# Chunk bounds with the keys held still and the queries streamed, and a scheduler with a table of priority shifts

## Chip, cores, metric

One core of a Trainium2 chip runs the whole program. The metric is device time in microseconds (us); a kernel's time is the median of its runs. The engines are TensorE (PE, with its weight loads shown apart as PEld), VectorE (DVE), ScalarE (ACT), GpSimd (POOL) and SyncE (SP), which here only issues DMAs.

## What is computed

For 4 batches and 8 heads, sequence 768, head size 64, attention is restricted to 6 of 24 key chunks per query. The chunks are chosen by an upper bound from the chunk's minimum and maximum keys. The result feeds a phase mixer of width 512.

```python
k_min = np.min(k_chunks, axis=3)
k_max = np.max(k_chunks, axis=3)
ub = np.sum(np.maximum(q[:, :, :, None, :] * k_min[:, :, None, :, :], q[:, :, :, None, :] * k_max[:, :, None, :, :]), axis=-1)
ub = np.where(causal, ub, -1000000000.0)
top_chunks = np.argsort(ub, axis=-1)[..., -top_k:]
...
theta = x @ w_theta
zr = x * cos_t
zi = x * sin_t
yr = np.einsum('ts,bsd->btd', w_tok_r, zr)
yi = np.einsum('ts,bsd->btd', w_tok_i, zi)
u = x + (yr + yi)
return (u + np.maximum(u @ w_ch, 0.0))
```

## The kernel before, in words

The work of a batch falls into two groups of four heads, 8 groups in all. For one group:

- **tree** (`keys`, L334 to L342): DVE takes the maximum and the minimum of the keys of each chunk, in three steps each. PE transposes the two results (psk, L355) and DVE writes them with signs into the fp32 tile `bnd` (L360): for either sign `y`, a column per head and chunk, with zeros in the 64 rows that belong to the other head of a pair.
- **kext**: POOL casts the keys (L367), PE transposes them (pkt, L375), ACT or DVE copies them out (L381).
- **queries** (L404, L412, L414): PE transposes two heads' queries in fp32 (psq); ACT or DVE writes the positive and the negative part into `ubq`, fp32, for the 5 blocks of 128 queries that need a choice. The blocks come in two parts, of 2 and of 3 (`PARTS`).
- **choice** (L433 to L464): PE multiplies the queries by `bnd`. For each block, pair of heads and sign there is one fp32 matmul: the 128 query columns are the stationary operand, the 48 columns of `bnd` stream. The result, psub, has queries on its partitions. DVE adds the causal mask (ubs, L440), finds the 8 largest of 24 per head (L450) and writes the selection into `qe` (L455). Two transposing DMAs turn `qe` into `qext` (L464).
- **scores, av, norm** (L500 to L545) for each head: PE computes scores (psc), ACT the exponentials (pt), POOL the triangular mask, PE the product with the values (psav), DVE the division into `x16`.

A batch then has transposes of x16 (psT), **phases** (pst L590, cosine and sine on ACT L598, product zz on DVE L604), the **mixer** (psy, in the last batch also psz, L630 and L632: 12 matmuls of 512 columns for each of 6 token tiles; u on DVE L642) and the **output** (a transpose of u, on PE as psut L652 with a copy uT L656, or by DMA L646; pso L664; ot L669; a DMA to the output).

The kernel writes no order by hand. Each piece is a task with an engine (or two that may take it), a duration, a key and its buffers, and `Plan.order` plays the tasks through a list scheduler: whichever engine can start first takes, of the tasks that can start at once, the one with the smallest key. The program is emitted in that order, and each engine runs its instructions in it. `LAT` is the latency that the scheduler adds behind a task of an engine. PSUM has 2 buffers "sc" for scores, 1 "av" and 3 "mi"; psk, pkt, psq, psub, psT, pst, psy, pso and the rest share the three.

The matmul of the bounds is this:

```python
for a in range(nb):
    for z, u in enumerate(us):
        c = slice(z * 2 * NCH, (z + 1) * 2 * NCH)
        for y in range(2):
            nc.tensor.matmul(t[:, a, c], st[u][:, y, (i0 + a) * P:(i0 + a + 1) * P],
                             bnd[g][:, y, c], start=(y == 0), stop=(y == 1))
```

Of the kernel before, what the change touches and what calls it, by code (L numbers as in the profile page):

```python
# [16 lines left out]
class Task:  # L17
    __slots__ = ("i", "eng", "dur", "fn", "key", "deps", "succ", "alloc", "uses", "opts", "lock", "psum",
                 "after_start", "left", "ready", "start", "end", "kind")


class Plan:
# [8 lines left out]
    LAT = {"PE": 0.15, "ACT": 0.20, "DVE": 0.12, "POOL": 0.15, "SP": 2.0}  # L31

    def __init__(self, bufs, in_order, hot, boost):
        self.tasks = []
        self.bufs = bufs
        self.in_order = in_order
        self.count = {}
        self.hot, self.boost = hot, boost
        self.turn = {}
        self.writers, self.readers = {}, {}  # L40
        self.tag_of, self.users = {}, {}

    def add(self, eng, dur, key, fn, r=(), w=(), new=(), after=(), kind=None, lock=False):
# [3 lines left out]
        t.lock = lock or eng == "POOL"  # L47
        t.deps, t.after_start, t.succ, t.alloc, t.uses = set(), set(), [], [], []
# [142 lines left out]
def kernel(  # L191
# [41 lines left out]
    for t in range(2):  # L233
# [18 lines left out]
    bnd = [per.tile([P, 2, 96], FP32, name=f"bnd{i}", tag=f"bnd{i}") for i in range(2)]  # L252
# [8 lines left out]
        "v32": ([P, 2, NT, D], FP32, 2), "mm": ([96, 192], FP32, 1), "h1": ([96, 24, D], FP32, 1),  # L261
        "ubq": ([P, 2, NM * P], FP32, 4), "ubs": ([P, NM, 4, NCH], FP32, 1), "top8": ([P, NM, 4, 8], FP32, 1),
# [3 lines left out]
        "cs": ([P, 2, dm], FP16, 2), "ot": ([P, dm], FP32, 2),  # L266
    }
# [6 lines left out]
    plan = Plan({**{t: s[2] for t, s in SIZE.items()}, **PSUM}, set(SIZE), set(PSUM), BOOST)  # L274
# [24 lines left out]
    def load_kc(b, g, key):  # L299
        n = ("kc", b, g)  # L300

        for c in range(4):
# [4 lines left out]
            dma(key, 196608, 280, go, w=[(n, c)], nw=[n] if c == 0 else [])  # L307

    def load_q(b, p, key):
        n = ("q32", b, p)  # L310
# [6 lines left out]
    def load_v(b, g, y, key):  # L317
        n = ("v32", b, g, y)
# [8 lines left out]
    def keys(b, g, key, wait, lead):  # L327
        kc, mm, psk = ("kc", b, g), ("mm", b, g), ("psk", b, g)
        rk = [(kc, c) for c in range(4)]
        for i, op in ((0, ALU.max), (1, ALU.min)):  # L330
# [5 lines left out]
            def quarter(op=op, hn=hn):  # L336
                h1 = st[hn]
                nc.vector.tensor_tensor(out=h1[:, 16:24, :], in0=h1[:, 0:8, :], in1=h1[:, 8:16, :], op=op)  # L338

            def red(i=i, op=op, hn=hn):  # L340
                t = new(mm) if i == 0 else st[mm]
                nc.vector.tensor_reduce(out=t[:, i * D:(i + 1) * D],  # L342
                                        in_=st[hn][:, 16:24, :].rearrange("p w d -> p d w"), axis=AX.X, op=op)
# [6 lines left out]
        plan.add("POOL", 0.25, key - 0.5, dup, r=[(mm, 0)], w=[(mm, 2)])  # L350
# [8 lines left out]
        def ev():  # L359
            nc.vector.tensor_tensor(  # L360
                out=bnd[g].rearrange("p i (h j c) -> p i h j c", h=4, c=4),
                in0=st[psk].rearrange("p i (c h j) -> p i h j c", c=4, h=4),
                in1=signs[:, 2:194].rearrange("p (i h j c) -> p i h j c", i=2, h=4, c=4), op=ALU.mult)
        plan.add("DVE", dve_t(192), key, ev, r=[(psk, 0), "signs"], w=[("bnd", g)])
        for a in (0, 16):
            def cast(a=a):
                nc.gpsimd.tensor_copy(out=ke[:, a:a + 16, :], in_=st[kc][:, a:a + 16, :])  # L367
            plan.add("POOL", 1.1, key, cast, r=rk, w=[("ke", a)])
# [19 lines left out]
    def queries(b, p, key):  # L388
        q32, g, x0 = ("q32", b, p), p // 2, 2 * (p % 2)
# [5 lines left out]
        plan.add("POOL", 0.9, key, cast, r=rq + ["qe0"], w=[("qe", x0, "q")])  # L395
# [24 lines left out]
    def choice(b, g, key):  # L420
        ubs, top8 = ("ubs", b, g), ("top8", b, g)
        for i, blocks in enumerate(PARTS):
# [4 lines left out]
            def mm(i0=i0, nb=nb, psub=psub, us=us):  # L427
                t = newp(psub, "mi", [P, nb, 4 * NCH], FP32)
                for a in range(nb):
                    for z, u in enumerate(us):  # L430
                        c = slice(z * 2 * NCH, (z + 1) * 2 * NCH)
                        for y in range(2):
                            nc.tensor.matmul(t[:, a, c], st[u][:, y, (i0 + a) * P:(i0 + a + 1) * P],  # L433
                                             bnd[g][:, y, c], start=(y == 0), stop=(y == 1))
            plan.add("PE", 0.13 * 4 * nb, key, mm, r=[("bnd", g)] + [(u, i, z) for u in us for z in range(2)],
                     w=[(psub, 0)], new=[(psub, "mi")])

            def add(i0=i0, nb=nb, psub=psub, i=i):
                t = new(ubs) if i == 0 else st[ubs]
                nc.vector.tensor_tensor(out=t[:, i0:i0 + nb], in0=st[psub].rearrange("p a (x c) -> p a x c", c=NCH),  # L440
                                        in1=cmask32[:, i0:i0 + nb].unsqueeze(2).broadcast_to([P, nb, 4, NCH]),
                                        op=ALU.add)
            plan.add("DVE", dve_t(nb * 96), key, add, r=[(psub, 0), "cmask"], w=[(ubs, i)],
# [27 lines left out]
    def values(b, g, key):  # L471
        for y in range(2):
# [10 lines left out]
    def attend(b, h, key, act_after):  # L483
        g, x = h // 4, h % 4
# [38 lines left out]
        psav = ("psav", b, h)  # L523
        for i, ts in enumerate(([0, 1, 2], [3, 4], [5])):
# [11 lines left out]
        rec, xx = ("rec", b, h), ("x16", b)  # L536
        rp = [(psav, i) for i in range(3)]
# [18 lines left out]
    def transpose16(src, dst, c, key, reads, by_dma):  # L556
        pst = ("psT",) + dst + (c,)
        if by_dma:
            def tp():
                if c == 0:  # L560
                    new(dst)
                nc.sync.dma_start_transpose(out=st[dst][:, c, :].rearrange("p (a t) -> p a t", t=P),
                                            in_=st[src][:, :, c * P:(c + 1) * P].rearrange("p a d -> p (a d)"))
            raise NotImplementedError

# [13 lines left out]
    def phases(b, key, act_after):  # L579
        xx, xT, zz = ("x16", b), ("xT16", b), ("zz", b)  # L580
        act = []
# [228 lines left out]
```

## Time and profile before

| | |
|---|---|
| median of 3 runs | 307.36 us (306.66 to 308.02) |
| the profiled execution | 305.35 us |
| its span on the core | 303.5 us |
| PE busy | 262.7 us, 87% |
| DVE busy | 194.2 us, 64% |
| ACT busy | 152.7 us, 50% |
| POOL busy | 134.7 us, 44% |
| mean share of the DMA engines, queue 1 | 60.9% |

The span runs from the first to the last instruction that the profiler saw; the execution's own time is 1.85 us longer. Busy time of PE counts the modelled length of matmuls that overlap, so it is an upper reading. Shares over the span hide that the program has parts with different limits: loads and trees at first, the attention of the first two batches with the weights' loads, then two batches with few loads, and a last mixer with nothing beside it.

### The profile page before, as it was taken

Reading aid. Unit: us, or ns where it says so; the run is one execution under the profiler, and the core shown is the slowest. Engines: PE = TensorE matmul, PEld = TensorE weight load, DVE = VectorE, ACT = ScalarE, POOL = GpSimd, SP = SyncE. Lnnn points to the kernel's source line nnn. Section 1 sums busy time; section 2 is a strip of 40 time slices with the busy share of each in tenths; the row PEclk is TensorE's granted clock in tenths of the full one; section 3 lists DMA queues with packets and bytes.
Section 4 is the critical chain, followed back from the end, with each engine's and each line's share of the span. In section 5 each row is a group of like instructions: output and inputs, shape, how many; then the busy total and the mean of one; then the engine's idle time right before and its main releaser. Section 6 shows DMA issues by size and latency. Waiting matters only on the chain.

```text
span 303.5 us, 5732 instructions
## 1 busy us (share of the span) xinstructions
PE 262.7 (87%) x2168; PEld 181.6 (60%) x2168; DVE 194.2 (64%) x460; ACT 152.7 (50%) x213; POOL 134.7 (44%) x179
## 2 busy tenths in 40 slices
PE   0279599998699799899989699999999999889993
PEld 0169397697487357786675256866784676544441
DVE  0854925967968996968987825873776344443083
ACT  0421723776525498912545876915539875543010
POOL 2641254976854756987440435917300555200000
PEclk9999999999986999999997979999999999999999
DMA  7991794994996999899799414337207222110014
GB/s 133 200 187 36 129 186 79 240 195 87 250 210 180 245 258 212 237 220 188 199 201 197 112 54 105 51 74 147 62 2 174 37 75 66 54 52 35 0 47 163
DMA packets 90611, 40.81 MB, mean 134 GB/s; under 512 B 83880, under 2 KB 84136, under 8 KB 89816
## 3 DMA queue, kind: packets, MB, share of 16 engines
q1 hardware_dynamic: 90584, 40.45, 60.9%
q8 instruction: 17, 0.28, 0.4%
q14 instruction: 10, 0.08, 0.1%
HBM read 26.28 MB, written 6.29 MB: 107 GB/s over the span
## 4 chain that ended last, share of the span: by engine, by line
PE 62%; DVE 20%; DMA 6%; ACT 6%; issue 2%; POOL 2%; SPq 0%; DVEq 0%; POOLq 0%; ACTq 0%
PE psub L433 15%; PE psc L500 10%; PE psy L630 6%; PE psy L632 6%; PE psav L530 6%; PE pso L664 5%; DVE h L338 4%; PE pst L590 4%; DVE h L334 4%; DVE mm L342 3%; ACT pt L509 3%; DMA kc<-in_k_dram 2%; DVE zz L604 2%; PE psT L571 2%; DVE ot L669 2%
## 5 line engine op out<-in xcount | busy, mean ns | idle before, releaser
L509 ACT ACTIVATE pt<-psc 128x1024 f16<-128x1024 f32 (+1 forms) x96 | 82.8, 917 | 47.2 <-PE psc L500 46.2
L520 POOL TENSOR_TENSOR pt<-pt,tri 128x256 f16<-128x256 f16 x96 | 66.8, 711 | 60.8 <-ACT pt L509 60.6
L500 PE MATMUL psc<-qext,kext 88*128 88x512 f16 (+3 forms) x256 | 55.7, 337 | 8.5 <-DMA qext<-qe 4.2
L500 PEld LDWEIGHTS <-kext 88*128 88x128 f16 x256 | 34.2, 154 | 23.0 <-issue 12.6
L630 PE MATMUL psy<-zz,wtokT 128*128 128x512 f16 x120 | 46.5, 387 | 1.3 <-ACT cs L598 1.0
L433 PE MATMUL psub<-bnd,ubq 128*128 128x48 f32 x320 | 46.7, 314 | 0.8 <-DVE ubq L414 0.6
L433 PEld LDWEIGHTS psub<-bnd,ubq 128*128 128x128 f32 x320 | 46.0, 232 | 1.7 <-PE psc L500 0.8
L632 PE MATMUL psy<-zz,wtokT 128*128 128x512 f16 x120 | 46.4, 387 | 0.0
L530 PEld LDWEIGHTS <-pt 128*128 128x128 f16 x672 | 28.7, 101 | 5.2 <-issue 0.4
L530 PE MATMUL psav<-v,pt 128*128 128x65 f16 x672 | 30.3, 197 | 0.1
L664 PE MATMUL pso<-wch,uT 128*128 128x512 f16 x96 | 24.8, 389 | 4.0 <-DMA uT<-u 1.7
L412 ACT ACTIVATE ubq<-psq,signs 128x256 f32<-128x256 f32 (+1 forms) x39 | 18.6, 523 | 18.2 <-DVE ubq L414 9.7
L334 DVE TENSOR_TENSOR h<-kc 96x1024 f32<-96x1024 f32 x16 | 20.8, 1300 | 9.1 <-DMA kc<-in_k_dram 8.9
L404 PE MATMUL psq<-ident,q 128*128 128x128 f32 x80 | 15.8, 317 | 11.6 <-DMA q<-in_q_dram 10.3
L590 PE MATMUL pst<-wtheta,xT 128*128 128x512 f16 x96 | 23.8, 389 | 2.1 <-ACT cs L598 1.7
L669 DVE SCALAR_TENSOR_TENSOR ot<-pso,u 128x512 f32<-128x512 f32 x24 | 16.4, 689 | 14.1 <-PE pso L664 11.9
L367 POOL CAST ke<-kc 96x1024 f16<-96x1024 f32 x16 | 18.3, 1159 | 12.9 <-DMA kc<-in_k_dram 9.6
L440 DVE TENSOR_TENSOR ubs<-psub,cmask 128x192 f32<-128x192 f32 (+1 forms) x16 | 6.5, 407 | 27.2 <-PE psub L433 27.2
L598 ACT ACTIVATE cs<-pst,pi 128x512 f16<-128x512 f32 x24 | 16.9, 705 | 13.4 <-PE pst L590 7.3
L632 PEld LDWEIGHTS <-wtokT 128*128 128x128 f16 x144 | 14.3, 99 | 15.4 <-issue 3.7
L604 DVE TENSOR_TENSOR zz<-x,cs 128x1024 f16<-128x1024 f16 x24 | 19.2, 813 | 6.4 <-ACT cs L598 6.4
L630 PEld LDWEIGHTS <-wtokT 128*128 128x128 f16 x144 | 14.3, 99 | 13.9 <-issue 1.2
(49 smaller groups left out, 340.4 us busy)
## 6 DMA issues: line engine op xcount, KB each, us to landing
kc<-in_k_dram SPq DMA_DIRECT2D x32, 192.0 KB
q<-in_q_dram SPq DMA_DIRECT2D x32, 192.0 KB
v<-in_v_dram SPq DMA_DIRECT2D x64, 96.0 KB
out_dram<-ot SPq DMA_DIRECT2D x24, 256.0 KB
w<-in_moe_w_tok_r_dram SPq DMA_DIRECT2D x6, 384.0 KB
w<-in_moe_w_tok_i_dram SPq DMA_DIRECT2D x6, 384.0 KB
w<-in_moe_w_theta_dram SPq DMA_DIRECT2D x4, 256.0 KB
w<-in_moe_w_ch_dram SPq DMA_DIRECT2D x4, 256.0 KB
```

The lines of the kernel that those rows point to most:

```text
L334: nc.vector.tensor_tensor(out=new(hn)[:, 0:16, :], in0=st[kc][:, 0:16, :], in1=st[kc][:, 16:32, :], op=op)
L433: nc.tensor.matmul(t[:, a, c], st[u][:, y, (i0 + a) * P:(i0 + a + 1) * P], bnd[g][:, y, c], start=(y == 0), stop=(y == 1))
L500: nc.tensor.matmul(t[:, a0:a1], kx[0:KX, hj:CH * 96:NCH], qx[0:KX, q0 + a0 - o:q0 + a1 - o], start=True, stop=True)
L509: nc.scalar.activation(out=t[:, BASE[s]:BASE[s] + wa + wb], in_=st[psc][:, 0:wa + wb], func=AF.Exp, bias=0.0, scale=scale)
L520: nc.gpsimd.tensor_tensor(out=d, in0=d, in1=tri16.unsqueeze(1).broadcast_to([P, 2, P]), op=ALU.mult)
L530: nc.tensor.matmul(t[:, a, :], st[pt][:, o:o + P], v16s[g][:, x, j, :], start=(j == 0), stop=(j == a))
L590: nc.tensor.matmul(p, st[xT][:, c, t * P:(t + 1) * P], wtheta16[:, c, :], start=(c == 0), stop=(c == 3))
L604: nc.vector.tensor_tensor(out=st[zz][:, t, :, :], in1=st[cs], op=ALU.mult, in0=st[xx][:, t, :].unsqueeze(1).broadcast_to([P, 2, dm]))
L630: nc.tensor.matmul(acc(), wtokT16[:, i, 0, t * P:(t + 1) * P], st[zz][:, i, 0, :], start=(i == 0), stop=False)
L632: nc.tensor.matmul(acc(), wtokT16[:, i, 1, t * P:(t + 1) * P], st[zz][:, i, 1, :], start=False, stop=(i == NT - 1))
L664: nc.tensor.matmul(p, st[uT][:, c, :], wch16[:, c, :], start=(c == 0), stop=(c == 3))
L669: nc.vector.scalar_tensor_tensor(out=new(ot), in0=st[pso], scalar=0.0, op0=ALU.max, in1=st[u][:, t, :], op1=ALU.add)
```

## The change

Four edits.

1. The matmul of the bounds changes sides. `bnd` becomes a tile with 32 columns per head, of which 24 are used and 8 stay zero (a memset at the start). For each part, pair of heads and sign, 64 columns of `bnd` are the stationary operand and the part's 256 or 384 query columns stream. One pair of heads writes PSUM partitions 0 to 63, the other 64 to 127. A group has 8 such matmuls where it had 20.
2. The result now has chunks on its partitions, so it is copied to SBUF in fp32 (`ubm`, by ACT or DVE), transposed on PE in blocks of 128 (`psut` in `choice`, 5 for a group), and the mask is added from there.
3. Every task belongs to a named stage of a batch and group, and a table SHIFT adds a number to its key. Five latencies and several durations of the scheduler change. So the order of the whole program changes.
4. The tile h1 of the tree shrinks from 24 to 16 rows of chunks: its second step writes over its first rows.

```diff
-    LAT = {"PE": 0.15, "ACT": 0.20, "DVE": 0.12, "POOL": 0.15, "SP": 2.0}
+    LAT = {"PE": 0.22, "ACT": 0.08, "DVE": 0.08, "POOL": 0.08, "SP": 2.0}
...
+        t.key += self.shift.get(self.group, 0.0)
+        t.group = self.group
...
-    bnd = [per.tile([P, 2, 96], FP32, name=f"bnd{i}", tag=f"bnd{i}") for i in range(2)]
+    bnd = [per.tile([P, 2, 4, 32], FP32, name=f"bnd{i}", tag=f"bnd{i}") for i in range(2)]
...
+    SHIFT = {
+        ('av', 0, 0): 12.75, ('av', 0, 1): 16.25, ('av', 1, 0): -4.25, ('av', 1, 1): 2, ('av', 2, 0): 0.25,
...
-            dma(key, 196608, 280, go, w=[(n, c)], nw=[n] if c == 0 else [])
+            dma(key, 196608, 172, go, w=[(n, c)], nw=[n] if c == 0 else [])
...
-                nc.vector.tensor_tensor(out=h1[:, 16:24, :], in0=h1[:, 0:8, :], in1=h1[:, 8:16, :], op=op)
+                nc.vector.tensor_tensor(out=h1[:, 0:8, :], in0=h1[:, 0:8, :], in1=h1[:, 8:16, :], op=op)
...
+            c0, w = i0 * P, nb * P
+            ubm, psut = ("ubm", b, g), ("psut", b, g, i)
+
+            def mm(c0=c0, w=w, psub=psub, us=us):
+                t = newp(psub, "mi", [P, w], FP32)
+                for y in range(2):
+                    for z, u in enumerate(us):
+                        nc.tensor.matmul(t[64 * z:64 * z + 64, :],
+                                         bnd[g][:, y, 2 * z:2 * z + 2, :].rearrange("p x c -> p (x c)"),
+                                         st[u][:, y, c0:c0 + w], start=(y == 0), stop=(y == 1))
...
+            def cp(e, c0=c0, w=w, psub=psub, i=i):
+                t = new(ubm) if i == 0 else st[ubm]
+                (nc.scalar.copy if e == "ACT" else nc.vector.tensor_copy)(out=t[:, c0:c0 + w], in_=st[psub])
...
+            def tr(i0=i0, nb=nb, psut=psut):
+                t = newp(psut, "mi", [P, nb, P], FP32)
                 for a in range(nb):
...
+                    nc.tensor.transpose(t[:, a, :], st[ubm][:, (i0 + a) * P:(i0 + a + 1) * P], ident32)
...
+                nc.vector.tensor_tensor(
+                    out=t[:, i0:i0 + nb], in0=st[psut].rearrange("p a (x c) -> p a x c", c=32)[:, :, :, 0:NCH],
+                    in1=cmask32[:, i0:i0 + nb].unsqueeze(2).broadcast_to([P, nb, 4, NCH]), op=ALU.add)
...
+        for i in range(2):
+            nc.vector.memset(bnd[i], 0.0)
```

Three places show how the order moves. The first is PE at the bounds of the second group of batch 0 (psub from `bnd_76`). Before:

```order
L355 MATMUL psk<-ident_58,mm 128x96 x2
L500 LDWEIGHTS kext_67
L500 MATMUL psc<-qext_69,kext_67 128x512
L500 LDWEIGHTS kext_67
L500 MATMUL psc<-qext_69,kext_67 128x256
L500 LDWEIGHTS kext_67
L500 MATMUL psc<-qext_69,kext_67 128x256
L433 MATMUL psub<-bnd_76,ubq 128x48 x20
L530 LDWEIGHTS pt
L530 MATMUL psav<-v_0_73,pt 128x65
```

Now:

```order
L566 MATMUL psc<-qext_69,kext_67 128x384
L484 MATMUL psub<-ubq,bnd_76 64x256 x4
L484 MATMUL psub<-ubq,bnd_76 64x384 x4
L499 MATMUL psut<-ident_58,ubm 128x128 x2
L566 LDWEIGHTS kext_67
L566 MATMUL psc<-qext_69,kext_67 128x512
L566 LDWEIGHTS kext_67
L566 MATMUL psc<-qext_69,kext_67 128x128
L566 LDWEIGHTS kext_67
L566 MATMUL psc<-qext_69,kext_67 128x512
```

Twenty fp32 matmuls are replaced by eight wider ones and by transposes; scores of heads stand between the transposes of the first part and those of the second, while in the first group of all (not shown) the five transposes stand directly behind the eight matmuls.

The second is DVE at the same place. Before:

```order
L360 TENSOR_TENSOR bnd_76<-psk,signs 128x192
L440 TENSOR_TENSOR ubs<-psub,cmask_61 128x192
L450 MAX top_372<-ubs 128x8 x8
L455 TENSOR_TENSOR qe<-ubs,top_372 128x2x4x24
L440 TENSOR_TENSOR ubs<-psub,cmask_61 128x288
```

Now:

```order
L407 TENSOR_TENSOR bnd_76<-psk,signs 128x8x24
L492 COPY ubm<-psub 128x256
L381 TENSOR_TENSOR h_365<-kc 96x1024
L504 TENSOR_TENSOR ubs<-psut,cmask_61 128x192
L514 MAX top_391<-ubs 128x8 x8
L504 TENSOR_TENSOR ubs<-psut,cmask_61 128x288
```

The copy of the first part and a tree step of the next batch stand between `bnd` and the first mask; the copy of the second part stands on ACT, among exponentials. Of the 16 copies, 5 are on DVE (256 columns each) and 11 on ACT (3 of 256, 8 of 384).

The third is DVE at the end of the program, in the last mixer (u from psz and psy is the mixer's result, uT the copy of its transpose, ot the output). Before:

```order
L604 TENSOR_TENSOR zz<-x_2921,cs 128x1024 x2
L642 TENSOR_TENSOR u_3567<-psz,x_2921 128x512 x4
L642 TENSOR_TENSOR u_3567<-psy,x_2921 128x512 x2
L669 SCALAR_TENSOR_TENSOR ot<-pso,u_3567 128x512
L656 COPY uT_3678<-psut_3671 128x512
L656 COPY uT_3691<-psut_3680 128x512
L669 SCALAR_TENSOR_TENSOR ot<-pso,u_3567 128x512 x2
L656 COPY uT_3721<-psut_3715 128x512
L669 SCALAR_TENSOR_TENSOR ot<-pso,u_3567 128x512 x3
```

Now:

```order
L705 TENSOR_TENSOR u_3528<-psz,x_2948 128x512 x2
L720 COPY uT_3599<-psut_3592 128x512
L705 TENSOR_TENSOR u_3528<-psz,x_2948 128x512
L733 SCALAR_TENSOR_TENSOR ot<-pso,u_3528 128x512
L720 COPY uT_3625<-psut_3616 128x512
L733 SCALAR_TENSOR_TENSOR ot<-pso,u_3528 128x512 x2
L705 TENSOR_TENSOR u_3528<-psz,x_2948 128x512
L720 COPY uT_3671<-psut_3664 128x512
L705 TENSOR_TENSOR u_3528<-psy,x_2948 128x512
L733 SCALAR_TENSOR_TENSOR ot<-pso,u_3528 128x512
L705 TENSOR_TENSOR u_3528<-psy,x_2948 128x512
L720 COPY uT_3715<-psut_3705 128x512
```

Before, all six u come first and all six outputs last; now token tiles finish one after the other, and four of the six outputs' matmuls stand on PE ahead of the mixer's last matmul.

## Rows read from the trace of the kernel before

**Rows 1.** The page, sections 1 and 2: busy time of the engines; granted TensorE clock in 40 slices.

```profile
PE 262.7 (87%) x2168; PEld 181.6 (60%) x2168; DVE 194.2 (64%) x460; ACT 152.7 (50%) x213; POOL 134.7 (44%) x179
...
PEclk9999999999986999999997979999999999999999
```

**Rows 2.** The page, section 4: the chain that ended last, by engine and by line.

```profile
PE 62%; DVE 20%; DMA 6%; ACT 6%; issue 2%; POOL 2%; SPq 0%; DVEq 0%; POOLq 0%; ACTq 0%
PE psub L433 15%; PE psc L500 10%; PE psy L630 6%; PE psy L632 6%; PE psav L530 6%; PE pso L664 5%; DVE h L338 4%; PE pst L590 4%; DVE h L334 4%; DVE mm L342 3%; ACT pt L509 3%; DMA kc<-in_k_dram 2%; DVE zz L604 2%; PE psT L571 2%; DVE ot L669 2%
```

**Rows 3.** Windows of all engines: stretch, length, busy us (instructions), granted clock, DMA share.

```profile
48.00:62.00 14.00, 12.95 (x109) 8.88 (x108) 12.29 (x27) 10.01 (x12) 10.70 (x12) 1.00 0.74 161
...
89.00:96.00 7.00, 7.00 (x45) 5.73 (x45) 3.44 (x18) 2.29 (x3) 3.58 (x6) 0.52 0.78 210
96.00:126.00 30.00, 26.76 (x264) 17.64 (x263) 26.24 (x41) 23.67 (x33) 20.10 (x25) 1.00 0.97 229
...
156.00:179.00 23.00, 20.01 (x109) 11.51 (x108) 16.96 (x44) 14.36 (x22) 4.95 (x6) 0.85 0.69 138
...
227.00:262.00 35.00, 34.96 (x294) 21.08 (x293) 17.09 (x32) 26.69 (x36) 13.59 (x21) 1.00 0.31 76
```

**Rows 4.** Windows of psub alone: length, PE, PEld, DVE busy, granted clock.

```profile
17.00:30.00 13.00, 8.97 (x40) 8.72 (x40) 0.82 (x2) 1.00 0.62 102
39.00:49.00 10.00, 8.61 (x40) 8.64 (x40) 0.82 (x2) 1.00 0.90 167
...
85.00:93.00 8.00, 5.95 (x40) 5.79 (x40) 0.81 (x2) 0.74 0.92 211
...
220.00:226.00 6.00, 4.62 (x40) 4.54 (x40) 0.81 (x2) 1.00 0.01 3
sum 60.00, PE 46.75 PEld 45.93 DVE 6.37; mean PE 5.84 PEld 5.74 DVE 0.80
```

**Rows 5.** The chain in order of time: start, us, engine, tile, line, instructions.

```profile
24.04 5.13 PE psub L433 x24
...
39.71 8.40 PE psub L433 x40
...
62.62 0.55 PE psq L404 x5
...
220.49 4.45 PE psub L433 x40
```

**Rows 6.** Timeline of the end: start, us, engine, instruction [idle before <-releaser].

```profile
290.14 0.38 PE L630 MATMUL psy<-zz,wtokT 128*128 128x512 f16 x1
...
290.35 0.38 PE L632 MATMUL psy<-zz,wtokT 128*128 128x512 f16 x1
...
291.12 1.28 DVE L642 TENSOR_TENSOR u<-psy,x 128x512 f16<-128x512 f32 x2
...
291.86 0.38 PE L652 MATMUL psut<-ident,u 128*128 128x128 f16 x4 [0.26 <-DVE u L642]
...
296.44 0.42 DVE L656 COPY uT<-psut 128x512 f16<-128x512 f16 x1 [0.59 <-PE psut L652]
...
296.85 1.90 PE L664 MATMUL pso<-wch,uT 128*128 128x512 f16 x8 [0.51 <-ACT uT L656]
...
299.89 0.69 DVE L669 SCALAR_TENSOR_TENSOR ot<-pso,u 128x512 f32<-128x512 f32 x1 [1.16 <-DMA out_dram<-ot]
```

**Rows 7.** Groups by line and shape: busy us, mean ns of one, idle before.

```profile
L509 ACT ACTIVATE pt<-psc 128x1024 f16<-128x1024 f32 x64 | 62.7, 1022 | 36.1 <-PE psc L500 35.1 <-POOL pt L520 0.6
...
L412 ACT ACTIVATE ubq<-psq,signs 128x384 f32<-128x384 f32 x18 | 9.9, 581 | 7.8 <-DVE ubq L414 7.0 <-PE psq L404 0.8
L412 ACT ACTIVATE ubq<-psq,signs 128x256 f32<-128x256 f32 x21 | 9.0, 474 | 10.4 <-PE psq L404 7.7 <-DVE ubq L414 2.7
...
L414 DVE TENSOR_SCALAR ubq<-psq,signs 128x256 f32<-128x256 f32 x11 | 4.9, 475 | 0.0
```

**Rows 8.** Waits of DVE: who for whom, total us, times, longest us.

```profile
DVE ubs L440 <- PE psub L433: 27.2, 15, 3.8
```

More of the change, by code (lines that the diff above doesn't have):

```diff
@@ L273 @@
           for t, n in PSUM.items()}
-    plan = Plan({**{t: s[2] for t, s in SIZE.items()}, **PSUM}, set(SIZE), set(PSUM), BOOST)
+    plan = Plan({**{t: s[2] for t, s in SIZE.items()}, **PSUM}, set(SIZE), set(PSUM), BOOST, SHIFT)
     st = {}
@@ L299, in load_kc @@
     def load_kc(b, g, key):
+        plan.group = ("lk", b, g)
         n = ("kc", b, g)
@@ L317, in load_v @@
     def load_v(b, g, y, key):
+        plan.group = ("lv", b, g)
         n = ("v32", b, g, y)
@@ L324, in load_v, with keys @@
             dma(key, 98304, 180, go, w=[(n, c)], nw=[n] if c == 0 else [])
-    def keys(b, g, key, wait, lead):
+    def keys(b, g, key, wait):
+        plan.group = ("tree", b, g)
         kc, mm, psk = ("kc", b, g), ("mm", b, g), ("psk", b, g)
@@ L360, in ev @@
             nc.vector.tensor_tensor(
-                out=bnd[g].rearrange("p i (h j c) -> p i h j c", h=4, c=4),
+                out=bnd[g][:, :, :, 0:NCH].rearrange("p i h (j c) -> p i h j c", c=4),
                 in0=st[psk].rearrange("p i (c h j) -> p i h j c", c=4, h=4),
                 in1=signs[:, 2:194].rearrange("p (i h j c) -> p i h j c", i=2, h=4, c=4), op=ALU.mult)
-        plan.add("DVE", dve_t(192), key, ev, r=[(psk, 0), "signs"], w=[("bnd", g)])
+        plan.add("DVE", dve_t(192), key, ev, r=[(psk, 0), "signs", "bnd0"], w=[("bnd", g)])
+        plan.group = ("kext", b, g)
         for a in (0, 16):
@@ new lines, in choice @@
+            plan.add("PE", 8 * w * MM + 0.05, key, mm, r=[("bnd", g)] + [(u, i, z) for u in us for z in range(2)],
+                     w=[(psub, 0)], new=[(psub, "mi")])
+            def cp(e, c0=c0, w=w, psub=psub, i=i):
+                t = new(ubm) if i == 0 else st[ubm]
+                (nc.scalar.copy if e == "ACT" else nc.vector.tensor_copy)(out=t[:, c0:c0 + w], in_=st[psub])
+            plan.add({"ACT": act_t(w), "DVE": dve_t(w)}, None, key, cp, r=[(psub, 0)], w=[(ubm, i)],
+                     new=[(ubm, "ubm")] if i == 0 else [])
@@ L471, in values @@
     def values(b, g, key):
+        plan.group = ("values", b, g)
         for y in range(2):
@@ L483, in attend @@
     def attend(b, h, key, act_after):
+        plan.group = ("scores", b, h // 4)
         g, x = h // 4, h % 4
@@ L553, in attend, with transpose16 @@
         return act
-    def transpose16(src, dst, c, key, reads, by_dma):
+    def transpose16(src, dst, c, key, reads):
         pst = ("psT",) + dst + (c,)
[L558 to L564, printed above, removed]
+        plan.group = ("xT",) + dst[1:]
         def tr():
@@ L581, in phases @@
         act = []
+        plan.group = ("phases", b)
         for t in range(NT):
@@ L605, in z @@
                                         in0=st[xx][:, t, :].unsqueeze(1).broadcast_to([P, 2, dm]))
-            plan.add("DVE", 0.7, key, z, r=[(cs, 0), (cs, 1)] + [(xx, h) for h in range(H)], w=[(zz, t)], lock=True)
+            plan.add("DVE", 0.72, key, z, r=[(cs, 0), (cs, 1)] + [(xx, h) for h in range(H)], w=[(zz, t)], lock=True)
         return act
@@ L644, in mixer @@
             put, uT = ("psut16", b, t), ("uT16", b, t)
+            plan.group = ("out", b, t)
             if b in UDMA:
```

85 lines of the change are left out of this document (57 added, 28 removed), and 6 rows, old and new, of the table SHIFT.

## Prediction

> **What bounds the kernel now.** I read the page first: PE is busy 262.7 of 303.5 us, 87%, the next engine 64% [rows 1]. A share over the span says little by itself, so the chain of waits comes next: 62% of it is PE, 20% DVE, and the largest single line is psub, the bounds, with 15%, about 45.5 us [rows 2]. The windows then show where which limit holds [rows 3]. From 227 to 262 us PE is busy 34.96 of 35 us: there a microsecond taken off PE is a microsecond. From 96 to 126 PE is busy 26.76, DVE 26.24 of 30 us, and the DMA engines stand at 0.97: there what PE gives up can be taken by the other two.
>
> The windows of psub alone show what a group costs [rows 4]: 4.62 us late in the program, 5.95 us at 85 us, 8.97 and 8.61 us for the first two, 46.75 us in all. The 40 matmul records of a group are two passes for each of 20 fp32 matmuls. PEld is busy nearly as long as PE (4.54 of 4.62), though only 48 columns stream for 128 that are loaded: the block is paced by its weight loads. The chain gives the pace: 4.45 us for 40, so 0.11 us each, at 220 us; 8.40 for 40 and 5.13 for 24, so 0.21 us each, before 49 us [rows 5]. The same instruction at exactly twice the time is TensorE at 1.2 instead of 2.4 GHz. The clock row of the page reads full speed there [rows 1]; I believe the durations.
>
> **The change part by part.**
>
> *The blocks of the bounds.* A group now has 8 matmuls of two passes: 8 passes of 256 and 8 of 384 columns, 5120 columns, with only 64 weight columns to load for each pass, which the stream covers. What an fp32 column costs when the stream is the limit, no row shows. Below: fp16 matmuls of 512 columns follow each other at 0.21 us (290.14, 290.35) [rows 6], 0.41 ns a column, 2.10 us a group. Above: five fp32 transposes of 128 columns in 0.55 us [rows 5], 0.86 ns a column, 4.40 us; these are paced by weight loads too, so it is an upper end. The two pairs of heads use different halves of the array's columns; if their streams ran side by side, the upper price would again come down to 2.2 us. I take the middle, 3.25 us: the type is that of the upper row, but its load limit is gone. To this come 5 fp32 transposes at 0.11, 0.55 us. So 3.80 us a group (2.65 to 4.95) at the upper clock, twice that for the first two. After: 6 x 3.80 + 2 x 7.60 = 38.0 us for 46.75, which is -8.75 us (-20.25 to +2.75). Nearly all of psub is on the chain, but in the first half DVE and the DMA engines are close behind; I count two thirds: **-5.8 us**.
>
> The Trainium skill, "Perfetto Trace Analysis", section Engine Utilization, gives fp32 in two passes half the output rate, which would make a pass as fast as one in fp16. By that page a group would be at the lower end, 2.65 us; no row here shows it.
>
> *The clock.* From 89 to 96 us the granted clock is 0.52, so at 1.2 GHz, with PE busy throughout [rows 3]. It falls inside a psub block, whose clock is 0.74 [rows 4] and in which 48 columns stream in the time of 128. The new block streams without such holes, so I let this fall vanish: 7.0 x 0.48 = **-3.4 us**. Bounds: nothing; or also an earlier rise (12.95 us of PE work from 48 to 62 us at half the time, 6.5 us) and the falls from 156 to 179 (0.15 x 23 = 3.5 us), 13.4 us in all.
>
> *Copies.* 11 on ACT (3 x 0.474 + 8 x 0.581 = 6.1 us) and 5 on DVE (5 x 0.475 = 2.4 us) by the rows of ubq of the same widths [rows 7]. ACT has room in every window shown; scores on PE stand between most copies and their transposes. Not in the first group: there the transposes stand right behind the matmuls, the copy is on the only path to the first selection, and nothing covers it: 0.58 and some 0.2 of handing over, **+0.8 us**. If exponentials stand ahead of a copy, this becomes a rival below.
>
> *The end.* Before, the mixer's last matmul starts at 290.35, and 13.15 us follow to 303.5 [rows 6]. Now behind the last one stand its length 0.38, one u 0.64, one set of transposes 0.38, one copy 0.42, one pso 0.95, one ot 0.69, and 2.92 us from the last ot's end (300.58) to the span's end: 6.4 us. Ahead of it now stand four outputs (16 matmuls at 0.21, 3.4 us) and their transposes (0.2 each, 0.8). 13.15 - 6.4 - 4.2 = **-2.5 us** (0 if DVE's outputs pile up as before, -4 if the transposes hide).
>
> *The rest of the order.* Every queue is reordered, SP's too: the first selection's DMA now stands behind a quarter of the next batch's keys and no longer behind five value loads. That cannot be summed row by row. PE stands idle 3.2 us from 96 to 126 and 3.0 from 156 to 179 [rows 3]; I give the order a third of these 6.2, **-2 us**, with bounds +4 (new waits of that size) and -6.
>
> *At nothing:* the smaller h1 and the memset of `bnd`: same elements per DVE step, and the memset runs while DVE waits for the first keys.
>
> **Sum:** -5.8 - 3.4 + 0.8 - 2.5 - 2 = -12.9 us. The profiled execution took 305.35 us (span 303.5), so 292.4; the median of the runs is 2.0 above that execution, so **294.4 us** as a median.
>
> **Rivals.**
>
> 1. *Cheap columns and an early clock.* The lower price, -20.25 x 2/3 = -13.5 for -5.8, and some 2 us of an earlier rise, as ACT, busy 10 of 14 us from 48 to 62 [rows 3], would soon be the limit: 285 us. For it: halves that can run side by side; against: the DMA share of 0.97 in the middle.
> 2. *Dear columns.* At 4.95 us a group is slower than now at the upper clock: +1.8 for -5.8, so 302.0 us, carried by clock, end and order alone. For it: the only fp32 rows we have.
> 3. *Draining at the block's edges.* If PE must empty its pipe wherever 64-column and full-width work meet, each edge costs a matmul's length less its pace, 0.38 - 0.21 = 0.17 us [rows 6]. The order has 9 such blocks, 18 edges: 3.1 us, 297.5 us. The Trainium skill, "TensorEngine Tiling (Array Packing)", section Key Properties, says just that: changing the tiling mode drains TensorE. No row of the trace before shows a change of mode.
> 4. *A new wait takes the place of the old pace: slower.* PE runs in order. A transpose that waits for its copy holds all scores and mixer work behind it. The copy waits in turn behind an exponential of 1.02 us on ACT [rows 7], then takes 0.5: 1.5 us for each of 16 parts. DVE's waits for psub, 27.2 us in 15 cases [rows 8], show that this handover is already long. Psub and psut also take two of the three "mi" buffers at once. If half the parts lie open, 12 us, and columns are dear, 294.4 + 12 + 7.6 = 314 us. It turns the sign from about nine open parts on at my price (12.9 / 1.5), from four at the dear one. Against it: scores stand between in most groups.
> 5. *The freed time is not used.* PE gets shorter, but the trees on DVE (L334 to L342, 11% of the chain [rows 2]) and the loads hold the first 180 us; the rest gives 1 to 2 us either way: 306 to 308 us.
>
> **Chances.** Forecast 0.42, rival 1 0.17, rival 2 0.13, rival 3 0.10: faster by over 0.5% in 0.82 (0.5%, some 1.5 us, is about what a measurement of this kernel can tell from no change). Rival 5: 0.08 within 0.5%. Rival 4: 0.10 slower. The range leaves out rival 4 and the outer parts of rivals 1 and 5: 284 to 306 us.
>
> **What would show it.** Right: psub plus psut under 4 us a group late in the program, PEld far below PE in the block, no fall of the clock around a block, under 8 us from the mixer's last matmul to the end. Rival 2: passes of 384 columns spaced at 0.33 us. Rival 3: gaps at the edges alone. Rival 4: a large wait of PE for ubm among the waits. Wrong altogether: a total over 306 us with the blocks shorter, which would mean that PE was not the limit where the chain says so.

## The result and the profile after

| | before | after |
|---|---|---|
| median of the runs | 307.69 us (306.66 to 315.04) | 282.69 us (279.84 to 283.85) |
| ratio | | 0.918, interval 0.909 to 0.928 |
| profiled execution, its span | 305.35, 303.5 us | 279.84, 278.1 us |
| PE busy, PEld busy | 262.7, 181.6 us | 235.0, 145.7 us |
| DVE, ACT, POOL busy | 194.2, 152.7, 134.7 us | 191.9, 161.3, 133.5 us |

The change makes the kernel 25 us faster. The forecast was 294.4 us with a range from 284 to 306: the sign was right, the size was wrong, and the time lies just outside the range. Executions over 1.5% above the fastest of their kernel are left out of every ratio, but not of the medians.

The page after, sections 1 and 2, answers to [rows 1]:

```profile
PE 235.0 (84%) x2016; PEld 145.7 (52%) x2016; DVE 191.9 (69%) x463; ACT 161.3 (58%) x228; POOL 133.5 (48%) x179
...
PEclk9999669799879999999999999999999999999999
```

PE is busy 27.7 us less, and the span is 25.4 us shorter: nearly all that PE gave up came out of the span. The clock row now shows low levels only in the first 82 us. It reads full speed up to its first event, at 22.6 us; the spacing of the passes below shows the lower level until then. The chain that ended last, by engine and by line, answers to [rows 2]:

```profile
PE 53%; DVE 21%; DMA 13%; SPq 5%; ACT 4%; issue 2%; POOL 1%; DVEq 0%; ACTq 0%; POOLq 0%
PE psc L566 10%; PE psy L693 7%; PE psub L484 7%; PE psy L695 7%; PE pso L728 5%; PE psav L597 5%; DMA kc<-in_k_dram 4%; DMA uT<-u 3%; ACT pt L575 3%; DVE h L381 3%; DVE top L514 2%; DVE qe L519 2%; PE pst L652 2%; DVE h L385 2%; DMA qext<-qe 2%
```

The bounds fall from 15% of a chain of 303.5 us to 7% of one of 278.1, so from about 45 to 19 us. Four of the stretches of [rows 3] (stretch, length, busy us of PE, PEld, DVE, ACT and POOL, granted clock, DMA share, GB/s); the program is further on at the same time now, so the work in a stretch is not the same:

```profile
89.00:96.00 7.00, 7.00 (x63) 4.17 (x63) 5.13 (x10) 6.40 (x8) 4.29 (x7) 1.00 0.94 222
96.00:126.00 30.00, 28.00 (x301) 19.62 (x298) 23.37 (x68) 16.94 (x25) 22.75 (x33) 1.00 0.97 223
156.00:179.00 23.00, 22.26 (x195) 14.48 (x194) 19.53 (x70) 14.34 (x23) 12.97 (x18) 1.00 0.83 158
227.00:262.00 35.00, 33.89 (x283) 19.53 (x282) 16.65 (x30) 21.07 (x29) 8.39 (x13) 1.00 0.23 67
```

The clock of 0.52 from 89 to 96 us and of 0.85 from 156 to 179 us is gone, and PE is fuller in both middle stretches (28.00 for 26.76, 22.26 for 20.01). Three pieces of the chain in order of time (start, us, what), for [rows 5]:

```profile
18.97 4.11 PE psub L484 x16
...
60.35 2.31 PE psub L484 x16
...
212.74 2.31 PE psub L484 x16
```

A group's 16 passes take 2.31 us, where 40 passes took 4.45. The first block (18.97) runs at the lower clock nearly to its end: pairs of passes of 256 columns start 0.43 us apart there, 0.216 us in the later blocks. The same windows of psub alone as in [rows 4], for two late groups (PE, PEld, DVE and ACT busy):

```profile
60.00:63.00 3.00, 2.38 (x16) 1.06 (x16) 0.42 (x1) 0.30 (x1) 1.00 0.95 251
212.00:216.00 4.00, 2.37 (x16) 1.06 (x16) 0.42 (x1) 0.48 (x1) 1.00 0.17 35
```

PEld is busy 1.06 us under 2.37 of PE, where it was 4.54 under 4.62: the block is no longer paced by its weight loads.

### The profile page after: what moved, and what is told of

Its sections match the earlier page's. It is cut to its first block, busy times and chain, and to the rows that moved or that the text cites. A ratio compares the mean times of both kernels' runs of the same rounds, so it can differ in the third digit from the quotient of the medians.

```text
span 278.1 us, 5466 instructions
## 1 busy us (share of the span) xinstructions
PE 235.0 (84%) x2016; PEld 145.7 (52%) x2016; DVE 191.9 (69%) x463; ACT 161.3 (58%) x228; POOL 133.5 (48%) x179
## 4 chain that ended last, share of the span: by engine, by line
PE 53%; DVE 21%; DMA 13%; SPq 5%; ACT 4%; issue 2%; POOL 1%; DVEq 0%; ACTq 0%; POOLq 0%
PE psc L566 10%; PE psy L693 7%; PE psub L484 7%; PE psy L695 7%; PE pso L728 5%; PE psav L597 5%; DMA kc<-in_k_dram 4%; DMA uT<-u 3%; ACT pt L575 3%; DVE h L381 3%; DVE top L514 2%; DVE qe L519 2%; PE pst L652 2%; DVE h L385 2%; DMA qext<-qe 2%
## 5 line engine op out<-in xcount | busy, mean ns | idle before, releaser
L586 POOL TENSOR_TENSOR pt<-pt,tri 128x256 f16<-128x256 f16 x96 | 65.9, 702 | 35.3 <-ACT pt L575 34.9
L566 PE MATMUL psc<-qext,kext 88*128 88x512 f16 (+3 forms) x256 | 54.5, 334 | 5.4 <-ACT pt L575 2.6
L693 PE MATMUL psy<-zz,wtokT 128*128 128x512 f16 x120 | 45.5, 379 | 2.1 <-DVE zz L666 1.8
L695 PE MATMUL psy<-zz,wtokT 128*128 128x512 f16 x120 | 45.4, 379 | 0.0
L453 PE MATMUL psq<-ident,q 128*128 128x128 f32 x80 | 14.4, 298 | 17.9 <-DMA q<-in_q_dram 10.3
L415 POOL CAST ke<-kc 96x1024 f16<-96x1024 f32 x16 | 20.1, 1275 | 15.8 <-DMA kc<-in_k_dram 15.8
L728 PE MATMUL pso<-wch,uT 128*128 128x512 f16 x96 | 24.2, 379 | 2.7 <-DMA uT<-u 2.7
L733 DVE SCALAR_TENSOR_TENSOR ot<-pso,u 128x512 f32<-128x512 f32 x24 | 16.4, 687 | 13.6 <-PE pso L728 13.4
L443 POOL CAST qe<-q 128x768 f16<-128x768 f32 x16 | 14.7, 925 | 22.1 <-DMA qext<-qe 11.3
L695 PEld LDWEIGHTS <-wtokT 128*128 128x128 f16 x144 | 14.1, 98 | 16.3 <-issue 3.2
L484 PE MATMUL psub<-ubq,bnd 128*64 128x384 f32 (+1 forms) x128 | 22.4, 497 | 0.0
L666 DVE TENSOR_TENSOR zz<-x,cs 128x1024 f16<-128x1024 f16 x24 | 17.9, 762 | 5.6 <-ACT cs L660 5.4
L705 DVE TENSOR_TENSOR u<-psy,x 128x512 f16<-128x512 f32 x20 | 13.6, 686 | 9.8 <-PE psy L695 9.6
```

The lines of the kernel that those rows point to most:

```text
L484: nc.tensor.matmul(t[64 * z:64 * z + 64, :], bnd[g][:, y, 2 * z:2 * z + 2, :].rearrange("p x c -> p (x c)"), st[u][:, y, c0:c0 + w], start ...
L566: nc.tensor.matmul(t[:, a0:a1], kx[0:KX, hj:CH * 96:NCH], qx[0:KX, q0 + a0 - o:q0 + a1 - o], start=True, stop=True)
L586: nc.gpsimd.tensor_tensor(out=d, in0=d, in1=tri16.unsqueeze(1).broadcast_to([P, 2, P]), op=ALU.mult)
L693: nc.tensor.matmul(acc(), wtokT16[:, i, 0, t * P:(t + 1) * P], st[zz][:, i, 0, :], start=(i == 0), stop=False)
L695: nc.tensor.matmul(acc(), wtokT16[:, i, 1, t * P:(t + 1) * P], st[zz][:, i, 1, :], start=False, stop=(i == NT - 1))
L728: nc.tensor.matmul(p, st[uT][:, c, :], wch16[:, c, :], start=(c == 0), stop=(c == 3))
```

## Experiments

Eleven runs, in the order in which the questions came up. Ratios are to the kernel before, run on the same chip.

### Each half of the change alone

The first run keeps the new matmuls and the old scheduler numbers:

```diff
-    LAT = {"PE": 0.22, "ACT": 0.08, "DVE": 0.08, "POOL": 0.08, "SP": 2.0}
+    LAT = {"PE": 0.15, "ACT": 0.20, "DVE": 0.12, "POOL": 0.15, "SP": 2.0}
...
-        t.key += self.shift.get(self.group, 0.0)
+        t.key += 0.0
```

(and five durations, of the loads of keys, of three tasks on POOL and of zz, at their old values; of the latencies four differ, SP's does not). The order is what the old numbers make of the new tasks, so it is not task for task that of the kernel before. Expected:

> The new bounds (edit 1 and 2) under the scheduler of the kernel before: old latencies, old durations, no SHIFT. Theory A, the time came mostly from the blocks of the bounds (46.75 us of psub before, 22.4 of psub and some 5 of psut after) and from the earlier clock: 288 to 293 us. Theory B, it came mostly from the order: 299 us or more, the blocks then being shorter but the chain going through DVE and DMA instead. In both the clock should rise inside the first block, near 23 us, if dense streaming is what raises it; if it stays at half rate until 60 us, the order raised it.

The second keeps the new order and puts the old matmuls into it; their result needs no copy and no transposes, so these tasks issue nothing:

```diff
-                        nc.tensor.matmul(t[64 * z:64 * z + 64, :],
-                                         bnd[g][:, y, 2 * z:2 * z + 2, :].rearrange("p x c -> p (x c)"),
-                                         st[u][:, y, c0:c0 + w], start=(y == 0), stop=(y == 1))
+                            nc.tensor.matmul(t[:, a, 2 * z:2 * z + 2, :], st[u][:, y, c0 + a * P:c0 + (a + 1) * P],
+                                             bnd[g][:, y, 2 * z:2 * z + 2, 0:NCH], start=(y == 0), stop=(y == 1))
```

> The order of the changed kernel, task for task, with the old matmuls of the bounds in the place of the new ones; the copy and the transposes are left out, as the old form needs none. Theory A: 299 to 303 us, the order alone giving 5 to 8. Theory B: 290 us or less. The clock should stay low into the fifties if dense streaming of the new block raised it.

The third has the new matmuls, LAT and durations, and an empty table:

> The changed kernel with the table SHIFT emptied, so new bounds, new latencies and durations, but the old keys. If the searched table is worth what theory B says, 293 us or more, near bounds_only; if the latencies and durations did most of the reordering, within 3 us of the changed kernel's 282.7.

| | median us | ratio | PE busy us | PE idle us |
|---|---|---|---|---|
| before | 306.01 | 1 | 262.7 | 40.8 |
| new bounds, old order | 295.53 | 0.972 (0.964 to 0.981) | 242.5 | 50.7 |
| old bounds, new order | 299.07 | 0.980 (0.969 to 0.991) | 259.7 | 35.8 |
| new bounds, empty table | 299.74 | 0.983 (0.975 to 0.992) | 241.9 | 57.2 |
| the change, again (below) | 281.83 | 0.924 (0.918 to 0.931) | 235.0 | 43.1 |

(Busy and idle of PE come from the profiled execution and its span; those of the kernel before and of the change from the ones above.) The bounds alone give 2.8%, some 8.5 us; the order alone 2.0%, some 6 us; the two together 7.6 to 8.2%, 23 to 25 us. So some 8.5 to 10.5 us belong to neither: **the halves are worth more together than apart**. The two ratios multiply to 0.953, and to 0.934 with both at the lower ends of their intervals; the change has 0.918 and 0.924. The last two columns show how. With the old order, the bounds take 20.2 us off PE's busy time, and PE's idle time grows by 9.9: half is lost. With the new order PE's busy time falls by 24.7 us, from 259.7 to 235.0, and its idle time grows by 7.3.

What PE waits for names the place. PE's waits in the run with the old order (us in total, times, longest):

```profile
PE psc L566 <- DMA qext<-qe: 5.9, 4, 3.4
PE psk L402 <- DVE mm L389: 4.6, 1, 4.6
PE pst L652 <- ACT cs L660: 3.8, 4, 1.5
```

and in the change:

```profile
PE psc L566 <- DMA qext<-qe: 2.6, 2, 2.3
...
PE pst L652 <- ACT cs L660: 1.5, 2, 1.3
...
PE psk L402 <- DVE mm L389: 1.0, 1, 1.0
```

With the old order a faster block only brings PE sooner to work whose selection, tree or cosine is not there yet: 14.3 us of three waits against 5.1. Other waits go the other way (in the change PE waits 4.0 us once for ubq and 2.7 us for uT, which the old order doesn't have), so the idle time differs by 7.6 us only. That these waits are the whole of the interaction isn't shown; the run with the old order also spends more time at the lower clock (first rise at 26.6 us instead of 22.6, and 24 us behind it for 20, one fall as late as 286 us).

The third run says that the new latencies and durations by themselves give nothing (0.983 against 0.972 with the old ones): the order's gain sits in the table.

### Do the halves of the array run side by side?

In the change, matmuls of the two pairs of heads alternate. This run puts the two signs of one pair behind each other:

```diff
-                for y in range(2):
-                    for z, u in enumerate(us):
+                for z, u in enumerate(us):
+                    for y in range(2):
```

> The changed kernel with the same 8 matmuls of a group, but both signs of one pair of heads first, then both of the other, so that successive passes use the same half of the array's columns. If the two halves stream side by side only because they alternate, a block goes from 2.3 to about 4.0 us at the upper clock (7 turns for 4) and the kernel to 289 to 294 us; theory B says these 14 us lie beside other work and it stays under 286. If the halves overlap whatever the order, nothing changes.

It took 284.43 us, ratio 0.934 (0.927 to 0.942), 1.0 to 1.7% above the change's two ratios, with intervals that overlap. The blocks are nearly as long as before, 2.35 us for 2.31; the trace shows why. Passes start in pairs, mostly 6 or 7 ns apart in the change and 13 or 57 ns apart here, and the next pair 0.32 us later for 384 columns. The passes overlap in either order of the program. The records don't name the half of the array, so that a pair is one pass on each half, and not the two passes of one matmul, is argued: the program puts two passes of one half ahead of the other half's first in the change and four here, and the spacing in the pair grows from 6 or 7 to 13 ns, where two passes of one matmul would stand as close in either order. So this edit didn't take the overlap away, and another was needed: a stationary operand padded with zeros to 120 and 128 columns, so that both pairs of heads add into one full-width result.

```diff
-    bnd = [per.tile([P, 2, 4, 32], FP32, name=f"bnd{i}", tag=f"bnd{i}") for i in range(2)]
+    bnd = [per.tile([P, 2, 184], FP32, name=f"bnd{i}", tag=f"bnd{i}") for i in range(2)]
...
-                    for z, u in enumerate(us):
-                        nc.tensor.matmul(t[64 * z:64 * z + 64, :],
-                                         bnd[g][:, y, 2 * z:2 * z + 2, :].rearrange("p x c -> p (x c)"),
-                                         st[u][:, y, c0:c0 + w], start=(y == 0), stop=(y == 1))
+                    for z, u in ((1, us[1]), (0, us[0])):
+                        nc.tensor.matmul(t if z else t[0:120, :], bnd[g][:, y, 56:184] if z else bnd[g][:, y, 0:120],
+                                         st[u][:, y, c0:c0 + w], start=(y == 0 and z == 1),
+                                         stop=(y == 1 and z == 0))
```

> The changed kernel with the two pairs of heads no longer in two halves of the array: the stationary operand of either pair has 120 or 128 columns, zero where the other pair's heads belong, and all 4 matmuls of a part add up in one PSUM tile. Order and scheduler numbers as they are; DVE writes the keys' tile in two steps for one. If the two halves stream side by side, this doubles a block: 8 passes of 256 and 8 of 384 columns at 0.83 ns, 4.27 us for 2.31 at the upper clock. If PE's time in the blocks is what counts (theory A), 8 x 2 us and as much again for two blocks partly at half rate, so 296 to 302 us. If the dense stream and its clock count and not its length (theory C), 285 to 289 us. If the column is cheap and nothing runs side by side, no change.

It took 298.15 us, ratio 0.979 (0.973 to 0.985). Two of its blocks in the chain:

```profile
61.71 4.36 PE psub L487 x16
...
225.85 4.36 PE psub L487 x16
```

The same 16 passes take 4.36 us in single file and 2.31 us in pairs. 5120 columns in 4.36 us are 0.85 ns a column, the price of the prediction's upper row; in the trace one pass of 384 follows another after 0.322 us in both kernels. So a column costs the upper price, and two of them run at once. Against the change on the same chip, 281.83 us, the side-by-side passes are worth 16.3 us. PE's busy time differs by 14.6 us (249.6 in this run, 235.0 in the change) and the spans of the two profiled executions by 15.2 us (293.3 and 278.1): here a microsecond on PE is a microsecond. (DVE's second step for `bnd` costs it 1.2 us of busy time over the 8 groups.)

### The change again, the end, and the clock

> The changed kernel once more, on the same chip as the next three, so that these can be set against it directly: 280 to 285 us.

281.83 us, ratio 0.924 (0.918 to 0.931): the result stands. Next, the table without the mixer and the output of batch 3:

```diff
-        t.key += self.shift.get(self.group, 0.0)
+        t.key += 0.0 if self.group in TAIL else self.shift.get(self.group, 0.0)
```

with `TAIL = {(n, 3, t) for n in ("mix", "out") for t in range(6)}`.

> The changed kernel with the table's entries for the mixer and output of the last batch left out, which brings back the old order of the end (all six results first, all six outputs last) and leaves the rest. The prediction gave the end 2.5 us: 284 to 286 us. If the end is bound by PE either way, no change; if the interleaving also let the mixer start earlier, 5 us.

286.25 us, ratio 0.936 (0.927 to 0.945): by the two ratios 3.5 us slower than the change (4.4 by the medians). Their intervals overlap a little, so the size is loose; the forecast of 2.5 fits.

For the clock, fp16 matmuls whose result is overwritten fill PE's idle stretches at the start, in the change and in the kernel before. The one line of each kind that is added ahead of a psq:

```diff
+                for _ in range({(0, 0, 0): 40, (0, 1, 1): 20}.get((b, p, i), 0)):
+                    nc.tensor.matmul(t[:, 0:256], warm16[:, 0:P], warm16, start=True, stop=True)
```

> The changed kernel with matmuls on a constant fp16 tile in PE's idle stretches at the start: 40 of 256 columns ahead of the first queries, 20 ahead of the last part of the second pair's, 18 ahead of the first scores; their results are overwritten. If a dense stream raises the clock, it should stand at 2.4 GHz by 12 us in place of 22.6, the first block of the bounds take 2.3 us for 4.1, and the kernel 1 to 3 us less. If the first block's wait for DVE's tree sets the pace there, under 1 us. If the clock answers to something else, the rise stays at 22 us and the fillers cost up to 2 us.

> The kernel before, with 24 fp16 matmuls of 192 columns ahead of the first psk and 40 of 256 columns ahead of the first psq, on a constant, overwritten by what follows; the clock rises in the kernel before only at 61.6 us by the spacing of its passes. Theory A (the early clock is worth something by itself): the rise comes by about 6 us and holds through the first two psub blocks, which fall from 8.97 and 8.61 to about 4.6 us each; the loads hide part of it, ratio 0.975 to 0.99. Theory B (the old blocks themselves let the clock fall, as at 89 us): the rise comes early but the clock is at 1.2 GHz again within or right after the first block; ratio 0.99 to 1.005.

In the change: 283.26 us, ratio 0.918 (0.905 to 0.931), no difference from the change itself. The clock rose at 5.4 us already, was at the lower level again from 12.2 to 19.1 us, and fell from 29 to 40 and from 50 to 53 us as it does without the filling. In the 5 us ahead of the fall at 12.2 us PE was busy 1.77 us. In the kernel before: 305.09 us, ratio 0.992 (0.986 to 0.998). Its granted clock, and the first two blocks in its chain, one of them in two pieces:

```profile
PEclk9899555778699999959995999999989999999999
```

```profile
19.45 1.99 PE psub L438 x16
21.78 2.69 PE psub L438 x24
35.01 8.40 PE psub L438 x40
```

The first block ran at the upper clock, in 4.7 us for 8.97 [rows 4]; behind it the clock fell, from 30.4 to 57.7 us, and the second block took its 8.4 us again. (The mean granted clock is 0.87 to 0.91 in every execution of this run.) Of 4.3 us saved in the block about 2.5 us were left at the end. So an early clock is worth some 0.8% (0.2 to 1.4) in the old kernel and nothing measurable in the new one. The old kernel with the new order shows the same sequence late: a block of old bounds from 226.7 us, in which 40 loads of 128 columns feed 48 each, and then, from 230.2 us on, nearly 7 us at half the clock, with PE busy throughout (columns as in the windows above):

```profile
225.20:230.20 5.00, 5.00 (x41) 4.39 (x40) 0.69 (x1) 2.16 (x3) 2.01 (x3) 1.00 0.13 26
...
231.00:237.00 6.00, 6.00 (x39) 3.81 (x39) 1.48 (x4) 2.64 (x3) 1.71 (x3) 0.50 0.00 0
```

In the change no fall follows a block after 82 us. Its own three falls, at 29.4, 49.9 and 73.8 us, are of another kind: PE stood idle for about half of the time ahead of them.

```profile
24.40:29.40 5.00, 2.17 (x22) 1.52 (x19) 4.93 (x22) 4.76 (x8) 0.00 (x0) 1.00 0.29 55
44.90:49.90 5.00, 2.09 (x31) 1.63 (x30) 4.92 (x9) 3.78 (x5) 1.38 (x3) 1.00 0.39 72
68.80:73.80 5.00, 2.62 (x49) 2.27 (x50) 2.47 (x6) 1.64 (x3) 3.85 (x5) 1.00 1.22 125
```

The kernel before and the old bounds under the new order have three falls each ahead of their ends. Four of the six begin in or at the end of a block, with PE busy 4.46 to 5.00 of the 5 us ahead; two (at 174.2 and at 86.8 us) follow stretches with idle time, 2.87 and 3.20 of 5 us. The early rise goes with the new matmuls and not with the order: it comes at 22.6 to 26.6 us in the eight profiles that have them, no filling and a full clock, full width included, and at 59.5 us with the old ones under the new order.

### Parts of the table

Can the table's gain be put down to one chain of stages?

```diff
+    SHIFT = {k: x for k, x in SHIFT.items() if k[0] in ("lk", "lq", "tree", "kext", "queries", "choice")}
```

> The changed kernel, with the table cut to the stages that lead to the selection (loads of keys and queries, tree, kext, queries, choice); values, scores, av, norm, x transposes, phases, mixer and output have no shift. Without any table the ratio was 0.983, with all of it 0.924, so 18 us hang on the table. Theory A: the faster blocks pay only when the selection's chain (loads, tree, queries, choice, its DMA) runs earlier, so that PE no longer stands idle for qext (5.9 us of waits in bounds_only, 2.6 in the change) and for the tree's result (4.6 us against 1.0); then this run keeps most of it: 0.93 to 0.95. Theory B: the table pays through attention, mixer and output put between each other (the end alone was 4.4 us): 0.965 to 0.985.

318.06 us, ratio 1.042 (1.033 to 1.051). Both theories miss: with this half of the table the kernel is slower than before, and 18 us slower than with no table at all. PE's largest waits there, behind the first load:

```profile
PE psc L567 <- DMA qext<-qe: 8.9, 3, 6.3
PE pw L761 <- ACT cs L661: 5.1, 2, 4.8
PE psc L567 <- ACT pt L576: 4.3, 9, 1.2
PE psk L403 <- DVE rec L609: 4.3, 1, 4.3
```

PE waits 8.9 us for the selection's DMA, more than in the run without a table (7.2), though the selection's own stages carry their shifts. And the clock is at the lower level for 67 us of this span behind its first rise at 22.7 us (20 in the change, 34 without a table). The same for the loads alone:

```diff
+    SHIFT = {k: x for k, x in SHIFT.items() if k[0] in ("lk", "lq", "lv")}
```

> The changed kernel, with the table cut to the loads of keys, queries and values alone (SP's queue). If the order of the loads is what the table is worth: 0.94 to 0.955. If it is the order on the engines: within 1 % of the run without a table, 0.975 to 0.99.

299.61 us, ratio 0.982 (0.974 to 0.989), as without a table: the order of SP's queue alone is worth nothing. The complement of the selection's stages, and the stages of batches 2 and 3 alone, have no run. So what single entries of the table are worth stays open. Of the three parts that ran, the selection's stages alone lose time, the loads alone give nothing, and all but the end's entries keep most of the gain.

## Why the prediction was wrong in size

**What bounds the kernel** was read rightly: PE's busy time is what the end hangs on late in the program, and the block's load limit could be seen in PEld against PE.

**The blocks: a mis-sized term.** "I take the middle, 3.25 us" is the step that failed first. Measured: 2.31 us, and 0.55 us for five transposes where they stand together, as here in the chain of the change:

```profile
124.44 0.55 PE psut L499 x5
```

So 2.9 us a group, where the forecast was 3.80 and the lower bound 2.65. The sentence ahead of that step had the right pieces: the upper price for a column, and the halves side by side, "2.2 us". A mean of two bounds was taken where two mechanisms stood that could each be true or not; the dear price with overlap was one of the four cases, and the one that a layout with two separate halves of the array speaks for. In PE's busy time the blocks with their transposes went from 46.75 to 29.5 us (22.44 and 7.04), which is -17.3 and not -8.75. At two thirds that is 5.7 us more than the forecast counted, half of the 11.7 us by which it missed.

**The sum: terms that were not independent.** The forecast added the blocks, times two thirds, to the order. By the runs apart, -8.5 and -6 make -14.5 us, close to the forecast's -12.9. For the bounds alone (blocks, clock, copies: -8.4 by the forecast, -8.5 measured) that is luck: PE gave up more than forecast, and less of it was kept. The two thirds are no constant of the kernel: with the old order the bounds are worth 8.5 us of 20.2 that PE gave up (0.42), with the new order about 18 of 24.7 (0.7). The other half of the miss is here: the forecast has no term for what the order and the short blocks are worth together. Why the old scheduler numbers waste the short blocks isn't shown beyond the waits above; its plan had the new tasks with their own durations, so it was not a plan for long blocks.

**The clock.** The fall at 89 to 96 us vanished, as forecast at -3.4 us; what this alone was worth no run shows. The reason given, that the old block's short streams make it, agrees with the falls behind old blocks above, and with their absence behind new ones after 82 us; that no other cause takes part isn't shown. The falls from 156 to 179 us vanished too and the early rise came, both of which the forecast left to the bound of 13.4 us. The rise, at 22.6 instead of 61.6 us, was worth little: the 25th exponential starts at 75.7 us, where it started at 78.9, and the run that lifts the clock still earlier gains nothing. That loads and trees hold the start is argued, not shown.

**Copies.** PE's waits for ubm in the change are these:

```profile
PE pw L760 <- ACT ubm L492: 0.6, 1, 0.6
...
PE psut L499 <- ACT ubm L492: 0.2, 1, 0.2
```

0.8 us in all. Rival 4, with 12 us of them, is refuted.

**The end.** Forecast: 6.4 us from the last mixer matmul. Measured, by the timeline of the change (start, us, engine, instruction):

```profile
271.08 0.38 PE L695 MATMUL psy<-zz,wtokT 128*128 128x512 f16 x1
...
271.50 0.69 DVE L705 TENSOR_TENSOR u<-psy,x 128x512 f16<-128x512 f32 x1 [0.17 <-PE psy L695]
...
272.48 1.89 PE L728 MATMUL pso<-wch,uT 128*128 128x512 f16 x8
...
274.40 0.69 DVE L733 SCALAR_TENSOR_TENSOR ot<-pso,u 128x512 f32<-128x512 f32 x1 [0.17 <-PE pso L728]
```

7.0 us from 271.08 to 278.1, where 13.15 stood [rows 6]; two outputs are left behind the last matmul, as the forecast's own four ahead of it imply, while its sum counted one. From the last exponential's end to the span's end it is 38.7 us for 42.0, a gain of 3.3.

**The rest of the order.** Of the 6 us of the order alone, 2.5 (by the forecast) to 4.4 (from the last exponential to the end, 37.6 for 42.0 us) are the end's; the run without its shifts, 3.5, lies between. So 1.6 to 3.5 are left, and -2 was the term. Right in size, for the old blocks.

Where the gain lies in time (starts of the 1st, 25th, 49th and 73rd exponential, end of the last, end of the span; from the trace):

| | 1st | 25th | 49th | 73rd | last | end |
|---|---|---|---|---|---|---|
| before | 36.4 | 78.9 | 145.7 | 213.8 | 261.5 | 303.5 |
| new bounds, old order | 34.2 | 75.5 | 139.1 | 202.1 | 250.4 | 293.2 |
| old bounds, new order | 36.2 | 82.8 | 149.0 | 210.6 | 257.9 | 295.5 |
| the change | 31.7 | 75.7 | 138.3 | 197.0 | 239.4 | 278.1 |

Up to the 49th exponential the change is no further than the bounds alone; the extra gain comes behind it (5.1 us by the 73rd, 11.0 by the last), in the two batches with few loads, where PE is busy nearly all the time.

**The rivals.** *Rival 1* gave 285 us, the nearest: its block was nearly right (2.65 us for 2.9), by passes side by side and not by a cheap column, and its early clock wasn't the reason. *Rival 2* had the passes of 384 columns right (0.33 us by the prediction, 0.32 measured) and missed that two run at once. *Rival 3* was right in kind: behind the last pass of 384 the next matmul starts after 0.417 us in the change and after 0.323 in the full-width run, and the first pass follows the matmul ahead of it by 0.149 us against 0.055. So an edge costs about 0.094 us at the upper clock, 18 edges 1.7 us, half of the 3.1 that the rival gave. The Trainium skill, "TensorEngine Tiling (Array Packing)", section Key Properties, says that a change of tiling mode drains TensorE, and that tiles execute independently; the trace agrees with both, with 0.094 us an edge and with pairs 6 ns apart. *Rival 5* (the freed time not used) holds in part for the bounds under the old order, where 0.58 of what PE gave up is lost.

The half output rate for fp32 of the Trainium skill, "Perfetto Trace Analysis", section Engine Utilization, which the prediction took as a pass as fast as in fp16, does not hold in that reading: a pass costs 0.84 ns a column (384 in 0.322 us), twice the 0.41 ns of fp16 [rows 6]. Read as half the rate for each of the two passes, it agrees.

## What to carry to other kernels

When the price of an operation lies between two bounds because two mechanisms are unknown, forecast the combinations, not the middle. When a change makes one engine's work shorter and also reorders everything, don't add the two: time each half alone, and look at the idle time of the engine that was relieved, for if it grows, the order is the next limit. A table of priorities can't be judged by a part of it: the selection's entries alone were 12 to 13% slower here than the whole, and 6% slower than none.

## What the runs showed that was not expected

- fp32 passes of 64 columns run side by side in pairs even when the program puts the two matmuls of the same half behind each other: 16 passes take 2.31 us with the halves in turn, 2.35 us with one half ahead of the other, and 4.36 us without halves.
- An early rise of the clock didn't last: a clock at the upper level from 5.4 us on was at the lower level again from 12.2 us, and in the kernel with half of the table, whose PE waits most, some 67 us passed at the lower level. Ahead of its late falls (97.8, 162.6, 265.0 and 282.1 us) PE was busy 0.28 to 3.07 of 5 us, so waits stand ahead of the low clock; that they bring it is not shown by a run of its own.
